# Pooled attention with a layer-normed feed-forward: the last 128 keys multiplied on all rows, another order of heads, smaller pieces

## The chip, the cores and the metric

The kernel runs on 1 core of one Trainium2 chip. The metric is the device time of one execution in microseconds (us), as the median of several runs. The core has a matrix engine (TensorE, rows PE; its weight loads are PEld), VectorE (DVE), ScalarE (ACT), GpSimd (POOL) and an engine that only issues transfers (SP). PE writes its sums to PSUM, a memory of eight banks of 512 floats on each of 128 partitions; DVE and ACT take them from there.

## What is computed

Four batches of eight heads. Queries are averaged in pairs (1152 become 576), then comes ordinary attention with head size 64, and on its output (4 x 576 x 512) a feed-forward layer with layer norm and a residual:

```python
q_pool = q.reshape(B, H, S // 2, 2, D).mean(axis=3)
scores = scale * np.matmul(q_pool, k.transpose(0, 1, 3, 2))
attn = np.exp(scores - np.max(scores, axis=-1, keepdims=True))
attn = attn / (np.sum(attn, axis=-1, keepdims=True) + 1e-09)
x = np.matmul(attn, v)            # then heads side by side: 4 x 576 x 512
xn = (x - mu) / np.sqrt(var + 1e-06) * g_ln
out = x + np.maximum(xn @ w_ch1, 0.0) @ w_ch2      # 512 -> 2048 -> 512
```

Inputs and output are float32. A product of two float32 numbers is made of float16 halves: each factor is split in a high and a low part, and high x high, high x low and low x high are summed.

## The kernel before

**Tiles.** A batch has four pairs of heads (p = 0 to 15 in all), a pair nine score tiles (j = 0 to 8, C = 9), so there are 144 score tiles of 128 queries by 1152 keys. Tile j of a pair belongs to head 0 for j under 4, to head 1 for j over 4; tile 4 holds the last 64 queries of both heads. The output rows of a batch are gathered in `xb[b]`, four groups (t = 0 to 3) of 128 rows by 512 columns; group t needs tile t of each head, so it is whole when the batch's last pair has done its tile for head 1, which is j = 5 for t = 0, j = 6 for t = 1, up to j = 8 for t = 3. The rows of the j = 4 tiles of two batches share one more group (`xh`).

**One step.** `step(i)` writes the work on all engines by hand, in order: DVE's row maximum of tile i (L350), the exponential on ACT (L364), the scores of tile i+1 on PE (`emit_s`, L337), the split of the probabilities into high and low (ACT L378, DVE L387 or POOL L244 and L385), the product with V of an older tile on PE (L433), one piece that prepares the next pair's keys or queries (`a_prep`), and one portion of the feed-forward (`some_units`, at most one a step while tiles are left, two later). Engines run their lists in order.

**Scores.** Keys stand as `kt`, head size on the partitions: keys 0 to 511 of a head on rows 64 to 127, keys 512 to 1151 on rows 0 to 63 (queries `qt` stand on both halves). A tile is nine matmuls over 64 rows: three passes (high-high, high-low, low-high) of two 512-column products, whose two halves of the array run side by side, and then three 128-column products (keys 1024 to 1151) on rows 0 to 63 alone. They have the third bank of the tile's slot, which also holds small outputs, and wait for ACT to read those (L488). For j = 4 each is issued twice at 64 queries.

**The first batch** (`on_pe`, 36 tiles) transposes its probabilities on PE in float32 (L397) and multiplies with V in float32 (L421), while the weights arrive and are split by DVE, ACT and POOL. Later batches transpose by DMA from SP's queue (L390). While tiles of the first batch are worked on, `some_units` is not called.

**Feed-forward.** A whole group is normed (`ln_a`, `ln_r`: DVE L514, POOL L520 to L526), transposed on PE (L532) and split (ACT L538, DVE L539). When two groups (a half of a batch) are through, portions are queued: for each half of the hidden layer (w = 0, 1) four portions of the first product `l1` (L569, 24 matmuls of 256 columns, then ACT L582 and DVE L583 write `ht`), and for each of the two groups two portions of the second product `l2` (L600, 12 matmuls of 512 columns; after the second, DVE L614). So a batch has 32 portions, and the shared groups 8 for two batches.

**Names used below.** Block n is the stretch on PE from the first score matmul of the n-th tile (1 to 144) to that of the next; block 144 holds all that follows.

## Time and profile before

| | us |
|---|---|
| median of 3 runs (892.95 to 897.29) | 895.72 |
| the profiled execution, its own time | 892.43 |
| its span, first to last instruction | 890.6 |
| PE busy, share of the span | 94% |
| DVE, ACT, POOL busy, share of the span | 69%, 64%, 39% |

A row's busy time of PE counts a matmul from its start to its modelled end, and matmuls overlap; what one costs in a stream is the distance of two starts, or the time of a long run of them divided by their number. "Idle before" is time in which the engine waited, with what ended it. PEclk is the granted clock as a share of 2.4 GHz, so 0.50 is 1.2 GHz.

### The profile page before, as it was taken

The numbers are of one execution on the slowest core, as the hardware profiler recorded it, in microseconds if no ns is written. First come the engines' busy times: TensorE is split into PE (matmuls) and PEld (weight loads), VectorE is DVE, ScalarE is ACT, GpSimd is POOL, SyncE is SP. The second block draws the span as 40 slices with busy tenths as digits, with TensorE's granted clock in tenths as the row PEclk, the third lists the DMA queues.
The fourth block names the chain that finished last, engine by engine and source line by source line (L and its number), as shares of the span: only waits on it lengthen the run. The fifth ranks groups of instructions, "written<-read, shape, count | busy, mean of one in ns | idle before, by whom it ended". The sixth has DMA issues, their size and how long they took to land.

```text
span 890.6 us, 22107 instructions
## 1 busy us (share of the span) xinstructions
PE 837.2 (94%) x9430; PEld 608.2 (68%) x9430; DVE 611.8 (69%) x1094; ACT 568.4 (64%) x851; POOL 346.6 (39%) x316
## 2 busy tenths in 40 slices
PE   8898979899799999996999999998999999999997
PEld 6787768677566676754758576676667576776664
DVE  3586988888787777778777777787777777532211
ACT  4888788788677777776677777676767666211110
POOL 3010543543988844336435243535543422300000
PEclk9999999999899999997999999999999999999999
DMA  4554154403498779997896979895979778310001
GB/s 130 196 157 164 50 194 126 172 1 96 92 179 168 141 150 183 180 169 137 154 193 114 203 141 188 127 186 107 222 121 175 129 129 143 57 25 13 13 13 24
DMA packets 271667, 114.95 MB, mean 129 GB/s; under 512 B 254928, under 2 KB 254928, under 8 KB 271568
## 3 DMA queue, kind: packets, MB, share of 16 engines
q1 hardware_dynamic: 271216, 112.65, 61.4%
q8 instruction: 74, 1.21, 0.6%
q10 hardware_dynamic: 352, 0.88, 0.4%
q14 instruction: 25, 0.20, 0.1%
HBM read 45.09 MB, written 4.72 MB: 56 GB/s over the span
## 4 chain that ended last, share of the span: by engine, by line
PE 54%; DVE 25%; ACT 10%; DMA 5%; issue 3%; POOL 2%; SPq 1%; ACTq 0%; POOLq 0%; DVEq 0%
PE psum L569 15%; PE psum L600 15%; DVE mx L350 7%; PE psum L337 7%; PE psum L433 7%; DVE hl L387 4%; PE psum L421 4%; DVE stage L107 3%; ACT pe L364 3%; PE psum L397 2%; DVE ht L583 2%; DVE wsl L107 2%; DVE kt L270 2%; DMA qr<-in_q_dram 2%; DMA kr<-in_k_dram 1%
## 5 line engine op out<-in xcount | busy, mean ns | idle before, releaser
L350 DVE TENSOR_REDUCE mx<-psum 128x1 f32<-128x1152 f32 x144 | 194.2, 1349 | 27.1 <-PE psum L433 18.9
L364 ACT ACTIVATE pe<-psum,nb,sc 128x1152 f32<-128x1152 f32 x144 | 188.9, 1312 | 32.0 <-DVE nb L355 23.6
L600 PE MATMUL psum<-wsl,ht 128*128 128x512 f16 x864 | 196.0, 379 | 0.2 <-DVE ht L583 0.2
L569 PEld LDWEIGHTS <-wsl 128*128 128x128 f16 x1920 | 170.9, 98 | 22.7 <-issue 2.7
L569 PE MATMUL psum<-xn,wsl 128*128 128x256 f16 x1536 | 177.3, 274 | 1.9 <-DVE xn L539 1.0
L337 PE MATMUL psum<-kt,qt 64*128 64x512 f16 (+3 forms) x1440 | 151.8, 332 | 24.7 <-ACT xb L488 13.9
L337 PEld LDWEIGHTS <-qt 64*128 64x128 f16 (+1 forms) x1440 | 70.9, 98 | 116.0 <-issue 66.4
L600 PEld LDWEIGHTS <-ht 128*128 128x128 f16 x864 | 81.8, 98 | 90.0 <-issue 0.4
L378 ACT ACTIVATE hl<-pe 128x1152 f16<-128x1152 f32 x108 | 125.7, 1163 | 5.0 <-DMA pt<-hl 1.6
L433 PE MATMUL psum<-vt,pt 128*128 128x65 f16 (+1 forms) x3240 | 119.8, 195 | 0.0
L433 PEld LDWEIGHTS <-pt 128*128 128x128 f16 (+1 forms) x3240 | 108.1, 101 | 9.4 <-issue 0.6
L488 ACT ACTIVATE xb<-psum,r 128x64 f32<-128x64 f32 x128 | 39.7, 311 | 109.4 <-DVE r L484 100.1
L244 POOL TENSOR_SCALAR pe<-pe 128x1152 f32<-128x1152 f32 x36 | 41.9, 1164 | 164.0 <-ACT hl L378 153.7
L387 DVE SCALAR_TENSOR_TENSOR hl<-pe,hl 128x1152 f16<-128x1152 f32 x72 | 104.3, 1448 | 0.0
L582 ACT ACTIVATE ht<-psum 128x512 f16<-128x512 f32 x72 | 42.7, 594 | 90.6 <-PE psum L569 90.2
L583 DVE SCALAR_TENSOR_TENSOR ht<-psum,ht 128x512 f16<-128x512 f32 x72 | 49.6, 690 | 66.2 <-ACT ht L582 65.4
L385 POOL TENSOR_TENSOR hl<-pe,hl 128x1152 f16<-128x1152 f32 x36 | 86.4, 2400 | 3.0
L421 PE MATMUL psum<-pt,vt 128*65 128x128 f32 (+1 forms) x720 | 81.6, 271 | 0.0
L421 PEld LDWEIGHTS psum<-pt,vt 128*65 128x65 f32 x720 | 75.8, 144 | 0.2 <-issue 0.2
L270 DVE SCALAR_TENSOR_TENSOR qt<-psum,s,qt 128x384 f16<-128x384 f32 x48 | 29.6, 616 | 46.9 <-ACT qt L273 46.9
L270 DVE SCALAR_TENSOR_TENSOR kt<-psum,s,kt 128x512 f16<-128x512 f32 (+1 forms) x48 | 31.5, 658 | 39.1 <-ACT kt L273 39.1
L403 ACT COPY pt<-psum 128x512 f32<-128x512 f32 x72 | 44.9, 639 | 10.8 <-PE psum L397 5.5
(112 smaller groups left out, 925.6 us busy)
## 6 DMA issues: line engine op xcount, KB each, us to landing
stage<-in_moe_w_ch_dram SPq DMA_DIRECT2D x32, 512.0 KB, 5.5
kr<-in_k_dram SPq DMA_DIRECT2D x16, 576.0 KB, 4.7
qr<-in_q_dram SPq DMA_DIRECT2D x31, 288.0 KB, 6.2
vr<-in_v_dram SPq DMA_DIRECT2D x15, 576.0 KB, 4.9
out_dram<-xb SPq DMA_DIRECT2D x32, 128.0 KB, 2.4
pt<-hl SPq DMA_TRANSPOSE x108, 5.0
vr<-in_v_dram ACTq DMA_DIRECT2D x1, 576.0 KB, 6.5
out_dram<-xh SPq DMA_DIRECT2D x4, 128.0 KB, 3.5
```

Source lines behind the costliest of these rows:

```text
L270: nc.vector.scalar_tensor_tensor(lo, ps, s, hi, op0=ALU.mult, op1=ALU.subtract)
L337: nc.tensor.matmul(out=sp[o:o + w, c0:c0 + n], lhsT=qt[r:r + 64, qa, q0:q0 + w], rhs=kt[r:r + 64, ka, h, k0:k0 + n], start=(a == 0), stop= ...
L350: nc.vector.tensor_reduce(mx, st["s"], axis=AX.X, op=ALU.max)
L364: nc.scalar.activation(out=st["pe"], in_=st["s"], func=ACTF.Exp, scale=pair[i // C]["sc"][:, 0:1], bias=st["nb"],)
L378: nc.scalar.activation(out=hl[:, 0], in_=st["pe"], func=ACTF.Copy, scale=2.0 ** 15)
L385: nc.gpsimd.tensor_tensor(hl[:, 1], st["pe"], hl[:, 0], op=ALU.subtract)
L387: nc.vector.scalar_tensor_tensor(hl[:, 1], st["pe"], 2.0 ** 15, hl[:, 0], op0=ALU.mult, op1=ALU.subtract)
L421: nc.tensor.matmul(out=ps[0:65, q0:q0 + w], lhsT=vt[:, h, c], rhs=pt[:, 128 * u + q0:128 * u + q0 + w], start=(u == 0), stop=(u == C - 1),)
L433: nc.tensor.matmul(out=dst[:, 0:n], lhsT=lhsT, rhs=rhs, start=(u == 0 and lhsT is hi and n == 65), stop=(u == C - 1 and lhsT is lo), skip_ ...
L569: nc.tensor.matmul(out=ps[:, o:o + n], lhsT=wsl[:, 8 * w + cc, wa, f * 128:f * 128 + 128], rhs=xn[:, xa * KD + cc, 0:n], start=(m == 0), s ...
L583: lambda: nc.vector.scalar_tensor_tensor(lo, pv, 0.0, hi, op0=ALU.max, op1=ALU.subtract),
L600: nc.tensor.matmul(out=ps, lhsT=hv[0][:, ha, f, t * 128:t * 128 + 128], rhs=wsl[:, 8 * w + 4 + f // 2, wa, (f % 2) * DM:(f % 2) * DM + DM] ...
```

## The change

**Scores.** `kt` keeps 512 keys on each half; the last 128 keys get a place of their own, `k8`, on all 128 rows: rows 0 to 63 hold their high part, rows 64 to 127 their low part. One 128-column matmul over 128 rows then makes high-high and high-low at once, a second one with the queries' low part the rest: eight matmuls a tile for nine. The 512-column products are unchanged. To have the keys on both halves, `kr` gets a tenth column, a second copy of the ninth, with a load of its own on SP's queue (64 KB in runs of 256 bytes for each pair); the PE transpose turns both.

**Order of heads.** `PLACES` names the head and group of each j. In the first two pairs of a batch it is as before; in its last two pairs the heads take turns: (head, t) = (0,0) (1,0) (0,1) (1,1), the shared tile, (0,2) (1,2) (0,3) (1,3). Queries are transposed in that order, and keys of head 1 one place earlier (`PREPS`).

**Pieces.** For the first batch alone, the second product of the second group of each half is made in three portions of 8 matmuls, not two of 12.

**Also.** `all_max` takes its diagonal from the transposed values in PSUM, by one instruction as before.

```diff
+    PLACES = [[(h, t) for h in range(2) for t in range(4)], [(h, t) for t in range(4) for h in range(2)]]
+    for x in PLACES:
+        x.insert(C // 2, None)
...
+        if which == "k":
+            r = raw_p.tile([128, 2, C + 1, D], FP32, tag="kr", name="kr")
+            eng.dma_start(out=r[:, :, 0:C], in_=x)
+            eng.dma_start(out=r[:, :, C], in_=x[:, :, C - 1])
...
-            st["kt"] = tr_p.tile([128, 2, 2, 640], FP16, tag="kt", name="kt")
+            x = tr_p.tile([128, 2304], FP16, tag="kt", name="kt")
+            st["kt"] = x[:, 0:2048].rearrange("p (a h n) -> p a h n", a=2, h=2)
+            st["k8"] = x[:, 2048:2304].rearrange("p (h n) -> p h n", h=2)
...
         for h in range(2):
-            nc.tensor.transpose(ps[0:64, 128 * h:128 * h + 128], kr[:, h, C - 1], ident)
-        x = ps[0:64, 0:256].rearrange("p (h n) -> p h n", h=2)
-        return split_from((p, "k", 2), x, s[0:64, 0:1], kt[0:64, 0, :, 512:640], kt[0:64, 1, :, 512:640])
+            x = kr[:, h, C - 1:C + 1].rearrange("p c d -> p (c d)")
+            nc.tensor.transpose(ps[:, 128 * h:128 * h + 128], x, ident)
+        x = ps[:, 0:256].rearrange("p (h n) -> p h n", h=2)
+        k8 = pair[p]["k8"]
+
+        def low():
+            nc.vector.scalar_tensor_tensor(
+                k8[64:128], x[64:128], s[64:128, 0:1], k8[64:128], op0=ALU.mult, op1=ALU.subtract
+            )
+            have.add((p, "k", 2))
+
+        return (lambda: nc.scalar.activation(out=k8, in_=x, func=ACTF.Copy, scale=s[:, 0:1]), low)
...
-    PREPS = ((prep_k, 0), (prep_k, 2), (prep_q, 0), (prep_q, 1), (prep_k, 1), (prep_q, 2))
+    PREPS = ((prep_k, 0), (prep_k, 2), (prep_q, 0), (prep_k, 1), (prep_q, 1), (prep_q, 2))
...
-        wide = ((64, 0, 512, 0), (0, 512, 512, 0))
-        for here in (wide, ((0, 1024, 128, 512),)):
-            for a, r, c0, n, k0 in [(a, *x) for a in range(3) for x in here]:
-                ka, qa = ((0, 0), (1, 0), (0, 1))[a]
...
+        for a in range(3):
+            ka, qa = ((0, 0), (1, 0), (0, 1))[a]
+            for r, c0 in ((64, 0), (0, 512)):
                 for h, q0, w, o in parts:
                     nc.tensor.matmul(
...
+        for qa in range(2):
+            for h, q0, w, o in parts:
+                nc.tensor.matmul(
+                    out=sp[o:o + w, 1024:1152],
+                    lhsT=qt[:, qa, q0:q0 + w], rhs=pair[p]["k8"][:, h],
+                    start=(qa == 0), stop=(qa == 1),
+                )
...
-            (2 * w + 1, 2 + f0 // 2, lambda t=t, f0=f0: l2(t, f0))
-            for t in range(len(xs)) for f0 in (0, 4)
+            (2 * w + 1, (m1 + 5) // 6, lambda t=t, m0=m0, m1=m1: l2(t, m0, m1))
+            for t in range(len(xs))
+            for m0, m1 in (((0, 8), (8, 16), (16, 24)) if t and fine else ((0, 12), (12, 24)))
...
-                [[(64 * s, rows(b, 2 * x + s)) for s in range(2)] for x in (u, u + 1)],
+                [[(64 * s, rows(b, 2 * x + s)) for s in range(2)] for x in (u, u + 1)], b == 0,
...
-        key = ("h", b // 2) if j == 4 else (b, j if j < 4 else j - 5)
+        key = ("h", b // 2) if j == 4 else (b, PLACES[p % HP // 2][j][1])
```

Where the portions stand after the first batch shows on ACT, which writes `ht` once for each portion of the first product, and casts `xn` once for each normed group. One block is here from one `pe` to the next. Before, from the look at the third pair's values (blocks 39 to 42):

```order
L180 ACTIVATE kt,acc<-vr 128x1152
L916 ACTIVATE pt<-psum,nhalf 65x128
L538 CAST xn<-psum 128x4x128
L364 ACTIVATE pe<-psum,nb,sc 128x1152
L378 ACTIVATE hl<-pe 128x1152
L488 ACTIVATE xb<-psum,r 128x64
L538 CAST xn<-psum 128x4x128
L364 ACTIVATE pe<-psum,nb,sc 128x1152
L378 ACTIVATE hl<-pe 128x1152
L488 ACTIVATE xb<-psum,r 128x64
L273 ACTIVATE kt<-psum,s 128x512
L538 CAST xn<-psum 128x4x128
```

The same place in the changed kernel, from the same instruction on:

```order
L191 ACTIVATE kt,acc<-vr 128x1152
L948 ACTIVATE pt<-psum,nhalf 65x128
L613 ACTIVATE ht<-psum 128x512
L395 ACTIVATE pe<-psum,nb,sc 128x1152
L409 ACTIVATE hl<-pe 128x1152
L519 ACTIVATE xb<-psum,r 128x64
L613 ACTIVATE ht<-psum 128x512
L569 CAST xn<-psum 128x4x128
L395 ACTIVATE pe<-psum,nb,sc 128x1152
L409 ACTIVATE hl<-pe 128x1152
L519 ACTIVATE xb<-psum,r 128x64
L286 ACTIVATE kt<-psum,s 128x512
```

Two of the three casts have gone to earlier blocks, and a portion stands in each block: the first one is in block 40, where before it is in block 43.

The second place is after the first batch's portions (blocks 75 to 79). Before, again from the look at the values of the next pair:

```order
L180 ACTIVATE kt,acc<-vr 128x1152
L488 ACTIVATE xb<-psum,r 128x64
L364 ACTIVATE pe<-psum,nb,sc 128x1152
L378 ACTIVATE hl<-pe 128x1152
L488 ACTIVATE xb<-psum,r 128x64
L538 CAST xn<-psum 128x4x128
L364 ACTIVATE pe<-psum,nb,sc 128x1152
L378 ACTIVATE hl<-pe 128x1152
L488 ACTIVATE xb<-psum,r 128x64
L273 ACTIVATE kt<-psum,s 128x512
L538 CAST xn<-psum 128x4x128
```

And in the changed kernel:

```order
L191 ACTIVATE kt,acc<-vr 128x1152
L519 ACTIVATE xb<-psum,r 128x64
L395 ACTIVATE pe<-psum,nb,sc 128x1152
L409 ACTIVATE hl<-pe 128x1152
L519 ACTIVATE xb<-psum,r 128x64
L613 ACTIVATE ht<-psum 128x512
L395 ACTIVATE pe<-psum,nb,sc 128x1152
L409 ACTIVATE hl<-pe 128x1152
L519 ACTIVATE xb<-psum,r 128x64
L286 ACTIVATE kt<-psum,s 128x512
L613 ACTIVATE ht<-psum 128x512
L569 CAST xn<-psum 128x4x128
```

Before, blocks 75 to 79 have no portion and block 80 the next batch's first; in the changed kernel block 75 has the last piece of the first batch (8 matmuls of the second product), block 76 none, and blocks 77 to 80 one each.

## Rows read from the trace of the kernel before

**Rows 1.** The page: busy time by engine, and the granted clock in 40 slices.

```profile
PE 837.2 (94%) x9430; PEld 608.2 (68%) x9430; DVE 611.8 (69%) x1094; ACT 568.4 (64%) x851; POOL 346.6 (39%) x316
...
PEclk9999999999899999997999999999999999999999
```

**Rows 2.** Busy time by stretch: stretch, its length, engines, clock, DMA share, GB/s.

```profile
core 0: us, PE busy (x) PEld busy (x) DVE busy (x) ACT busy (x) POOL busy (x), PEclk, DMA share, GB/s
14.29:215.25 200.96, 179.34 (x1777) 150.16 (x1778) 161.63 (x262) 161.43 (x296) 64.88 (x52) 0.97 0.38 122
215.25:231.99 16.74, 10.56 (x108) 8.07 (x108) 15.64 (x34) 11.56 (x17) 13.33 (x17) 0.87 0.43 89
231.99:398.40 166.41, 163.72 (x1984) 112.33 (x1983) 122.61 (x221) 119.04 (x161) 105.69 (x77) 0.98 0.87 164
398.40:429.34 30.94, 23.14 (x282) 16.33 (x282) 23.86 (x50) 21.43 (x29) 20.37 (x28) 0.78 0.83 153
429.34:751.09 321.75, 314.47 (x3968) 216.73 (x3968) 241.60 (x440) 226.72 (x303) 129.55 (x113) 1.00 0.84 155
751.09:890.60 139.51, 134.79 (x1179) 94.21 (x1178) 41.84 (x73) 23.24 (x40) 7.97 (x17) 1.00 0.15 29
...
586.98:620.99 34.01, 31.51 (x480) 24.34 (x480) 26.78 (x52) 22.48 (x30) 18.53 (x24) 1.00 0.64 126
...
405.00:412.00 7.00, 6.37 (x61) 4.05 (x60) 5.32 (x14) 5.20 (x8) 6.00 (x9) 0.51 0.74 144
418.70:425.50 6.80, 5.52 (x47) 3.58 (x48) 5.63 (x9) 4.86 (x8) 5.30 (x4) 0.50 0.47 91
217.30:220.70 3.40, 3.22 (x16) 3.02 (x16) 3.04 (x9) 3.37 (x5) 1.29 (x3) 0.50 0.56 117
231.00:237.80 6.80, 5.82 (x49) 4.09 (x49) 5.07 (x10) 5.73 (x7) 6.43 (x9) 0.50 0.93 174
```

**Rows 3.** PE in order of time, one full block: start, length, instruction, count.

```profile
353.00 0.99 PE L337 MATMUL psum<-kt,qt 64*128 64x512 f16 x9
353.92 0.99 PE L433 MATMUL psum<-vt,pt 128*128 128x65 f16 x27
354.74 2.75 PE L600 MATMUL psum<-wsl,ht 128*128 128x512 f16 x12
```

**Rows 4.** The chain that ended last, in the tail: start, length, what.

```profile
781.08 2.68 PE psum L569 x48
...
844.28 10.48 PE psum L569 x96
854.76 10.36 PE psum L600 x48
```

**Rows 5.** Groups by form: busy us, mean ns of one, idle before.

```profile
L433 PE MATMUL psum<-vt,pt 128*128 128x65 f16 x1728 | 97.0, 194 | 0.0
...
L583 DVE SCALAR_TENSOR_TENSOR ht<-psum,ht 128x512 f16<-128x512 f32 x72 | 49.6, 690 | 66.2 <-ACT ht L582 65.4
...
L337 PE MATMUL psum<-kt,qt 64*128 64x128 f16 x384 | 42.6, 218 | 13.6 <-ACT xb L488 12.0 <-ACT xh L488 1.6
...
L270 DVE SCALAR_TENSOR_TENSOR kt<-psum,s,kt 64x256 f16<-64x256 f32 x16 | 7.6, 475 | 9.4 <-ACT kt L273 9.4
```

**Rows 6.** PE in order of time, the block of the first portion.

```profile
231.99 1.78 PE L337 MATMUL psum<-kt,qt 64*128 64x512 f16 x9 [3.67 <-ACT pe L364]
```

**Rows 7.** PE in order of time, blocks 77 to 80.

```profile
404.98 1.81 PE L337 MATMUL psum<-kt,qt 64*64 64x512 f16 x18 [2.82 <-ACT pe L364]
...
419.81 0.63 PE L287 MATMUL psum<-ident,kr 128*64 128x128 f32 x2 [3.92 <-DVE kt L270]
```

**Rows 8.** DMA issues: out<-in, count, KB each, median us to landing.

```profile
kr<-in_k_dram SPq DMA_DIRECT2D x16, 576.0 KB, 4.7
```

**Rows 9.** SP's queue in order of time.

```profile
351.19 0.52 SPq L117 DMA_DIRECT2D kr<-in_k_dram  x1
```

More of the change, by code (lines that the diff above doesn't have):

```diff
@@ L115, in load @@
         src = k if which == "k" else v
-        r = raw_p.tile([128, 2, C, D], FP32, tag=which + "r", name=which + "r")
-        eng.dma_start(out=r, in_=src[b, h:h + 2].rearrange("h (p c) d -> p h c d", c=C))
+        x = src[b, h:h + 2].rearrange("h (p c) d -> p h c d", c=C)
+        if which == "k":
+            r = raw_p.tile([128, 2, C + 1, D], FP32, tag="kr", name="kr")
+            eng.dma_start(out=r[:, :, 0:C], in_=x)
+            eng.dma_start(out=r[:, :, C], in_=x[:, :, C - 1])
+        else:
+            r = raw_p.tile([128, 2, C, D], FP32, tag="vr", name="vr")
+            eng.dma_start(out=r, in_=x)
         raws[p, which] = r
@@ L175, in bound @@
         else:
-            src = raws[p, which][o:o + n].rearrange("p a b d -> p (a b d)")
+            src = raws[p, which][o:o + n, :, 0:C].rearrange("p a b d -> p a (b d)")
             if junk is None:
                 junk = kt_of(p)[o:o + n].rearrange("p a h n -> p (a h n)")[:, 0:S]
+                junk = junk.rearrange("p (a n) -> p a n", a=2)
         m = "kqv".index(which)
@@ L324, in emit_s @@
         if j == 4:
-            parts = [(h, h * C * 64 + 512, 64, 64 * h) for h in range(2)]
+            parts = [(h, 128 * j + 64 * h, 64, 64 * h) for h in range(2)]
         else:
-            h = 0 if j < 4 else 1
-            parts = [(h, h * C * 64 + 128 * (j if h == 0 else j - 5), 128, 0)]
+            parts = [(PLACES[p % HP // 2][j][0], 128 * j, 128, 0)]
         for h, q0, w, o in parts:
@@ L472, in evac_pv @@
                 xb[b] = x_p.tile([128, 4, DM], FP32, tag="xb", name="xb")
[L473 removed]
+            h, t = PLACES[hp // 2][j]
             o, n, m = 0, 128, 1
[L475 removed]
+            x = xb[b][:, t, 128 * hp + 64 * h:128 * hp + 64 * h + 64]
         r = r[o:o + n, 0:m]
@@ L551, in flush, with half_of @@
             drip()
-    def half_of(w, xn, xs, stores, free=()):
+    def half_of(w, xn, xs, stores, fine=False):
         n = 128 * len(xs)
@@ L588, in half_of, with l2 @@
         acc = {}
-        def l2(t, f0):
-            if t == 0 and f0 == 4:
+        def l2(t, m0, m1):
+            if t == 0 and m0 == 12:
                 flush()
-            if f0 == 0:
+            if m0 == 0:
                 acc[t] = bank()
@@ L597, in l2 @@
             ps = acc[t]
-            for f in range(f0, f0 + 4):
-                for ha, wa in ((0, 0), (0, 1), (1, 0)):
-                    nc.tensor.matmul(
-                        out=ps,
-                        lhsT=hv[0][:, ha, f, t * 128:t * 128 + 128],
-                        rhs=wsl[:, 8 * w + 4 + f // 2, wa, (f % 2) * DM:(f % 2) * DM + DM],
-                        start=(f == 0 and ha == 0 and wa == 0),
-                        stop=(f == 7 and ha == 1),
-                    )
-            if f0 == 0:
+            for m in range(m0, m1):
+                f = m // 3
+                ha, wa = ((0, 0), (0, 1), (1, 0))[m % 3]
+                nc.tensor.matmul(
+                    out=ps,
+                    lhsT=hv[0][:, ha, f, t * 128:t * 128 + 128],
+                    rhs=wsl[:, 8 * w + 4 + f // 2, wa, (f % 2) * DM:(f % 2) * DM + DM],
+                    start=(m == 0), stop=(m == 23),
+                )
+            if m1 < 24:
                 return ()
@@ L1021, in tile_pooled_attention_moe @@
         nc.scalar.activation(
-            out=kt_of(0)[:, 0].rearrange("p h n -> p (h n)")[:, 0:C * D],
-            in_=raws[0, "k"][:, 0].rearrange("p c d -> p (c d)"), func=ACTF.Abs,
+            out=kt_of(0).rearrange("p a h n -> p (a h n)")[:, 0:C * D],
+            in_=raws[0, "k"][:, 0, 0:C].rearrange("p c d -> p (c d)"), func=ACTF.Abs,
             accum_out=st["acc"][:, 0:1],
```

26 lines of the change are left out of this document (13 added, 13 removed).

## The prediction

> **What bounds the kernel now.** I read the page first: PE is busy 94% of the span and no other engine over 69% [rows 1]. That is an average, so next the stretches [rows 2]. In blocks 43 to 74 and 81 to 143 PE is busy 163.72 of 166.41 and 314.47 of 321.75 us, both 98%: a microsecond taken from PE there comes off the time. The tail (from block 144) is PE alone too, 134.79 of 139.51; its long runs of the two products follow each other without a hole [rows 4]. PE is not the limit in three places. Blocks 1 to 39, the first batch's attention: PE 179.34 of 200.96. Blocks 40 to 42: PE 10.56 of 16.74, DVE 15.64 of it. Blocks 75 to 80: PE 23.14 of 30.94, DVE 23.86. In the last two PE has its scores and its product with V but no portion of the feed-forward: the first batch's are not there yet, or are used up while the second's wait for their norms. PE stands for ACT or DVE, 2.82 and 3.92 us at a time [rows 7], and 3.67 at the end of the first hole [rows 6]. After pauses of PE the granted clock is down: 0.51, 0.50, 0.50 and 0.50 in the last four stretches of [rows 2], 1.2 GHz, so that a score tile takes 1.78 us [rows 6] for 0.99 [rows 3]. Where PE has work, half of such a stretch is lost to it: 3.4 us of the last one.
>
> **A matmul's price.** Busy time of one doesn't price it: 218 ns for a 128-column score matmul [rows 5]. Starts do. A run of 48 matmuls of 128 columns takes 2.68 us, 56 ns each; 96 of 256 columns 10.48, 109 ns each; 48 of 512 columns 10.36, 216 ns each [rows 4]. The block of [rows 3] fits: 0.92 us from scores to the product with V is 3 x 0.216 + 3 x 0.056 = 0.82, and some 0.10 left over, where the matmuls go from 128 rows to 64 and back. A portion of the first product is 24 x 0.109 = 2.62 us, one of the second 12 x 0.216 = 2.59, a small one 8 x 0.216 = 1.73.
>
> The Trainium skill, page "Trainium Kernel Development and Optimization", section Performance Expectations, says that matmul busy time is a bad metric since matmuls are pipelined. This trace agrees: 160 matmuls fewer would be worth 160 x 0.218 = 34.9 us by their busy time and 9.0 by their starts.
>
> **Scores on all rows.** 160 matmuls of 128 columns go (1440 to 1280), one a tile, two half-wide ones for j = 4. I take 0.056 us a tile. The three old ones stand on rows 0 to 63 alone, nothing runs beside them, and a matmul over 128 rows costs the same 56 ns [rows 4]. The passage from 64 to 128 rows now lies before the short products, not behind them; it is one passage either way. Bounds: 0 (the passage costs 0.05 more in its new place) and 0.15 (it vanishes where the short products wait anyway). Both ends count in PE-bound blocks.
>
> **Its preparation.** Instructions stay one for one on PE, ACT and DVE; at worst the split on DVE costs twice, another 7.6 us over 16 pairs [rows 5], on an engine that is 69 to 75% busy where PE bounds. Nothing. The second load costs SP 0.5 us per pair [rows 9]; behind it stand that block's transposes of probabilities, whose reader on PE never waited (idle 0.0) [rows 5]. Nothing while that slack holds. The keys of head 1 are turned one block earlier, so `kr` comes free earlier: a gain, if any. The diagonal of `all_max` is one small instruction either way.
>
> **Order of heads, pieces.** Group 1 of a batch is whole three tiles earlier (j = 3 for 6), so its portions start three blocks earlier: block 40 for 43, block 77 for 80 (the order above). The first batch has 36 portions for 32 (four sets of 3 pieces for 2). Work is the same; what changes is how many blocks lie without any. By stretch:
>
> Blocks 40 to 42 gain three portions of the first product, 7.9 us. PE has 10.56 busy in 16.74, 3.22 of it at half clock [rows 2], so its own work at full clock is 9.0; two norm transposes of 0.5 move forward, which with the portions makes 15.9. DVE has 15.64; it loses the work of two norms and gains three halves of `ht` at 0.69 [rows 5]. So the portions nearly fill the hole and the stretch stays about as long, 16.5: **-0.2**. Bounds: -0.9, and +3 if they don't fit by a third.
>
> Blocks 43 to 74 lose 3 x 2.62 + 1.73 = 9.6 (the portions done before, and 8 matmuls that move behind), and 32 x 0.056 = 1.8; they gain a norm's transposes, 0.5. Of the 3.4 lost at half clock at their start I take half back, 1.7. Against it: in a dozen blocks with a small piece PE has 3.4 to 4 us of work, while DVE needs 122.6 / 32 = 3.8 on average [rows 2]. So DVE ends some of them: +2 (0 to 4). **-10.6** (-14.3 to -5, the latter without the scores' gain and the clock's).
>
> Blocks 75 to 80 gain the 9.6 back. PE's 23.14 holds 6.37 + 5.52 = 11.9 at half clock [rows 2], so it is 17.2 at full, 26.8 with the portions. DVE's 23.86 gains four halves of `ht`, 2.8, and loses about as much, since the norms now come every other block and not four in a row. I take 28 for 30.94: **-3** (-4 to +1).
>
> Blocks 81 to 143 keep one portion each: 63 x 0.056 = 3.5, and something of the 2.5 us in which PE idles around the next norms (586.98 to 620.99) [rows 2]: **-4** (-5 to -1).
>
> The tail has three portions fewer: **-8**. This is the surest term; the order gives the count, 600 for 672 matmuls of the first product.
>
> Blocks 1 to 39: at most 39 x 0.056 = 2.2 from the scores, a little more where the short products wait for L488; against it two norms moved in here, some 3 us of DVE, 1 of PE. **0** (-3 to +2.5).
>
> Sum: -0.2 - 10.6 - 3 - 4 - 8 = -25.8. From the profiled execution's own 892.43 that is 866.6. The median of the runs stands 3.3 above that execution, so 870 for the median. All best ends (-0.9, -14.3, -4, -5, -8, -3) give -35.2, 860; all worst (+3, -5, +1, -1, -8, +2.5) give -7.5, 888.
>
> **Rivals.** (1) The holes don't take the portions: DVE is at 93% in blocks 40 to 42 and 77% in 75 to 80, and a portion comes with work for DVE and ACT, behind which the next row maximum waits. For it: PE's waits there end on ACT and DVE [rows 6, 7]. Against it: the stretch from 586.98 has norms and portions together, and PE is busy 31.51 of 34.01. Price: +3 in the first hole, +4 in light blocks, +1 in the second, half the gain of the scores gone, 4: some 11 us less, 881 at the median.
>
> (2) The change doesn't shorten the score tile: a 128-row weight load must wait until both halves of the array are through, and the two short products cost as much as three. For it: 0.10 us of each block is already spent on such a passage. Against it: the product with V streams 27 such matmuls in 0.82 us, 30 ns each [rows 3]. Price: the 0.056 of 134 blocks or so, 7.5: 877.
>
> (3) Clock: if PE no longer pauses long in the two holes, the clock stays up, and stretch for stretch the best ends come true: 861. For it: PE had paused ahead of the slow stretches of both holes [rows 6, 7]. Against it: DVE still limits there.
>
> (4) Slower than before: the second load of keys delays the transposes by DMA. The DMA engines are busy 0.83 to 0.87 of blocks 43 to 143 [rows 2], and the load comes in the same short stretch as a load of keys, values and queries. Price: to lose 25.8 us and 4.5 more, PE must wait 2.5 us for each of the 12 loads that meet such transposes, beyond the slack that it has now. Against it: the load has a ninth of the bytes of the one beside it, which takes 4.7 us to land [rows 8]; even as much again for each pair would have to go past the slack. It decides only if the small runs cost several times what the long ones do. That gives 897 or more.
>
> On those runs the Trainium skill, page "DMA: Bandwidth & Descriptors", section Specifications, asks for 512 bytes or more per transfer and says that below this the engine reads, modifies and writes; the new load has 256. No row of this trace shows such a load of keys. By that rule rival (4) would gain, and the time would be 897 or more.
>
> **How the numbers follow.** Forecast, 870: 0.66. Rival (1), 881: 0.14. Rival (2), 877: 0.07. Rival (3), 861: 0.07. No change, where holes and scores both give nothing and only the tail's blocks move: 0.03. Rival (4): 0.03. The range 858 to 882 takes in the forecast's bounds and rivals (1) to (3) nearly whole, and leaves out the last two and the tails of the sum, under 2 in 10. A measurement of this kernel can tell about 0.5%, 4.5 us, from no change. Faster by more: the forecast and rivals (1) to (3), less a little, 0.93; within: 0.04; slower: 0.03.
>
> **What would show it.** In the changed kernel's trace: eight score matmuls in about 0.87 us from the first to the product with V; portions in blocks 40 to 42 and 77 to 79, with blocks 40 to 42 about as long as before; PE's first portion of the second batch some 11 us earlier against its old place plus the gains before it; a tail shorter by 8; fewer stretches at half clock. I am wrong if blocks 40 to 42 or 75 to 80 grow by several us, if light blocks end on DVE for more than 4 us in sum, if PE begins to wait for transposed tiles, or if a score tile still takes 0.92.

## The result, and the profile after

The changed kernel takes **885.85 us** in the median (4 runs, 883.11 to 887.93), the kernel before 896.5 beside it: ratio **0.9891**, 95% interval 0.9859 to 0.9923 (the two medians alone give 0.988). The sign was right, the size was not: 870 was forecast, 858 to 882 was the range, and 10.6 us came where 25.8 were expected. The profiled execution took 883.11 us (span 881.3), against 892.43 (890.6) before.

The page after the change, PE's busy time and the granted clock; they answer to [rows 1]:

```profile
PE 826.2 (94%) x9270; PEld 586.0 (66%) x9270; DVE 613.4 (70%) x1092; ACT 568.7 (65%) x851; POOL 348.7 (40%) x318
...
PEclk9999989999999999999999999999999999999999
```

PE's busy time fell by 11 us, and in this execution the clock is up from block 40 on. The same stretches as in [rows 2], after the change: blocks 1 to 39, 40 to 42, 43 to 74, 75 to 80, 81 to 143, and the tail. Columns as there.

```profile
core 0: us, PE busy (x) PEld busy (x) DVE busy (x) ACT busy (x) POOL busy (x), PEclk, DMA share, GB/s
15.34:214.32 198.98, 179.08 (x1744) 147.86 (x1744) 163.54 (x267) 161.84 (x298) 67.51 (x60) 0.96 0.40 127
214.32:231.78 17.46, 15.67 (x167) 12.33 (x167) 12.72 (x27) 13.01 (x18) 11.66 (x12) 1.00 0.55 103
231.78:398.31 166.53, 152.48 (x1874) 99.16 (x1874) 128.46 (x226) 116.23 (x156) 108.09 (x84) 1.00 0.83 159
398.31:428.65 30.34, 26.92 (x350) 19.87 (x350) 23.30 (x48) 23.52 (x33) 15.86 (x19) 1.00 0.89 157
428.65:750.00 321.35, 313.06 (x3898) 208.20 (x3898) 242.62 (x442) 226.52 (x300) 132.37 (x117) 1.00 0.85 157
750.00:881.30 131.30, 126.66 (x1106) 87.07 (x1105) 37.70 (x66) 22.56 (x39) 7.93 (x16) 1.00 0.15 32
```

The third row is the riddle: PE has 11.2 us less to do there (163.72 before) and the stretch is as long as before (166.41). PE stands for 14.0 us in it, where it stood for 2.7. Of the waits over 0.5 us, 11.2 us in sum (1.6 before), 7.3 end on DVE (2.79, 0.86, 0.88 and 1.17 in blocks 43, 46, 47 and 49, 1.57 in block 73) and 3.9 on ACT's look at the keys and values of the next pair (1.40 in block 50, 2.54 in block 68). Set against the terms of the prediction, all in profiled executions:

| blocks | forecast | measured |
|---|---|---|
| start of the first score | none | +1.1 |
| 1 to 39 | 0 | -2.0 |
| 40 to 42 | -0.2 | +0.7 |
| 43 to 74 | -10.6 | +0.1 |
| 75 to 80 | -3 | -0.6 |
| 81 to 143 | -4 | -0.4 |
| tail | -8 | -8.2 |
| sum | -25.8 | -9.3 |

Two terms hold the miss: 43 to 74, and the scores in 81 to 143.

**Where PE stands in block 68.** This is the longest wait for a load. First SP's queue: four loads of queries, then transposes, the keys and the values of the next pair.

```profile
338.53 2.68 SPq L421 DMA_TRANSPOSE pt<-hl  x1
341.26 2.86 SPq L137 DMA_DIRECT2D qr<-in_q_dram  x4
...
345.58 4.77 SPq L421 DMA_TRANSPOSE pt<-hl  x1
350.79 0.39 SPq L121 DMA_DIRECT2D kr<-in_k_dram  x1
...
351.81 4.50 SPq L421 DMA_TRANSPOSE pt<-hl  x1
356.36 0.58 SPq L125 DMA_DIRECT2D vr<-in_v_dram  x1
```

Then ACT, which looks for the largest key and value, and PE's turn of what it found (`all_max`, L207):

```profile
355.85 1.16 ACT L191 ACTIVATE kt<-kr 128x1152 f16<-128x1152 f32 x1 [2.26 <-DMA kr<-in_k_dram]
...
361.27 1.16 ACT L191 ACTIVATE kt<-vr 128x1152 f16<-128x1152 f32 x1 [0.42 <-DMA vr<-in_v_dram]
...
362.58 0.27 PE L207 MATMUL psum<-ident,acc 128*3 128x128 f32 x1 [2.54 <-ACT kt L191]
```

A transpose behind the query loads holds SP for 4.8 and 4.5 us where 2.7 did before them, so the keys are issued at 350.79. In the kernel before they were issued at 351.19 [rows 9], but there PE was 2.4 us further back: block 66 began at 353.00 [rows 3], after the change at 350.62. PE runs ahead, the loads do not. The blocks 64 to 68 themselves, after the change, each from one tile's scores to the next:

```profile
341.34:346.49 5.15, 5.15 (x78) 3.26 (x78) 4.59 (x8) 2.58 (x3) 1.69 (x2) 1.00 1.03 222
346.49:350.62 4.13, 4.13 (x50) 2.34 (x50) 2.48 (x5) 3.57 (x7) 2.58 (x2) 1.00 1.13 202
350.62:354.14 3.52, 3.52 (x45) 1.85 (x45) 2.92 (x3) 2.94 (x4) 3.46 (x2) 1.00 1.00 245
354.14:358.97 4.83, 4.56 (x60) 3.47 (x59) 4.72 (x9) 3.09 (x5) 0.59 (x1) 1.00 1.09 180
358.97:366.22 7.25, 4.71 (x69) 3.58 (x69) 3.16 (x10) 6.20 (x9) 3.65 (x3) 1.00 1.12 218
```

Blocks 66 and 68 before:

```profile
353.00:357.43 4.43, 4.43 (x50) 2.36 (x50) 3.85 (x6) 3.74 (x6) 3.02 (x2) 1.00 1.06 287
...
361.89:366.64 4.75, 4.65 (x71) 3.71 (x71) 2.85 (x7) 4.12 (x6) 1.70 (x2) 1.00 1.22 184
```

The last column but one is the DMA share: it is full, 1.00 to 1.13, in the blocks that small pieces have shortened to 3.5 and 4.1 us. (A packet counts where it starts, so a short stretch can show more than 1.) It was as full before, but PE then had 4.4 us of work in block 66 and stood for 0.1 us in block 68. DVE (4.59 of 5.15 and 4.72 of 4.83 us) and POOL (3.46 of 3.52) are near their limits in single blocks too, so three bounds lie close under PE's there; the one that PE waits for is in the last row.

**Where PE stands in blocks 43 to 49.** POOL, DVE and PE, in block 43 and then in block 48:

```profile
232.06 2.13 POOL L788 TENSOR_TENSOR wsl<-wsl 128x1024 f16<-128x1024 f32 x1
232.21 2.07 DVE L246 TENSOR_SCALAR s<-s 128x3 f32<-128x3 f32 x1
...
236.43 0.44 PE L301 MATMUL psum<-ident,kr 128*128 128x128 f32 x2 [2.79 <-DVE kt L283]
...
262.20 2.63 POOL L172 TENSOR_TENSOR qr<-qr 128x1152 f32<-128x1152 f32 x1
262.41 0.62 DVE L283 SCALAR_TENSOR_TENSOR qt<-psum,s,qt 128x384 f16<-128x384 f32 x1 [0.91 <-ACT qt L286]
262.94 3.10 DVE L418 SCALAR_TENSOR_TENSOR hl<-pe,hl 128x1152 f16<-128x1152 f32 x1
```

An instruction of three columns takes 2.07 us on DVE, from just after POOL's split of weights starts until it ends; the split of a tile takes 3.10 beside POOL's sum of queries and 1.35 where POOL is idle. PE's waits of 2.79, 0.86, 0.88 and 1.17 us in blocks 43, 46, 47 and 49 end on DVE; `bare` below shows how many of them go with POOL's splits.

**The score tile.** PE in order of time, first with the product with V behind the scores, then with a matmul of three rows:

```profile
350.62 0.82 PE L362 MATMUL psum<-kt,qt 64*128 64x512 f16 x6
351.38 0.29 PE L370 MATMUL psum<-kt,qt 128*128 128x128 f16 x2
351.50 0.98 PE L464 MATMUL psum<-vt,pt 128*128 128x65 f16 x27
...
366.22 0.82 PE L362 MATMUL psum<-kt,qt 64*128 64x512 f16 x6
366.98 0.29 PE L370 MATMUL psum<-kt,qt 128*128 128x128 f16 x2
367.19 0.38 PE L218 MATMUL psum<-dg,ones 3*128 3x3 f32 x2
```

0.88 us from the first score to the product with V, for 0.92 in [rows 3]: what was forecast. But 0.97 where L218 follows. The passage from 64 rows to 128 shows as well: 0.76 from the first wide matmul to the first short one, where three wide pairs of 0.216 are 0.65.

### The profile page after: what moved, and what is told of

Same layout as the page of the kernel before. It is cut to its first block, busy times and chain, and to the rows that moved or that the text cites. A ratio compares the mean times of both kernels' runs of the same rounds, so it can differ in the third digit from the quotient of the medians.

```text
span 881.3 us, 21831 instructions
## 1 busy us (share of the span) xinstructions
PE 826.2 (94%) x9270; PEld 586.0 (66%) x9270; DVE 613.4 (70%) x1092; ACT 568.7 (65%) x851; POOL 348.7 (40%) x318
## 3 DMA queue, kind: packets, MB, share of 16 engines
HBM read 46.14 MB, written 4.72 MB: 58 GB/s over the span
## 4 chain that ended last, share of the span: by engine, by line
PE 47%; DVE 24%; ACT 11%; DMA 6%; issue 6%; POOL 4%; SPq 1%; ACTq 0%; POOLq 0%; DVEq 0%
PE psum L600 15%; PE psum L632 13%; DVE mx L381 7%; PE psum L464 5%; PE psum L362 4%; DVE hl L418 4%; PE psum L452 3%; ACT pe L395 3%; DVE stage L109 3%; DMA qr<-in_q_dram 2%; PE psum L428 2%; DVE ht L614 2%; DVE wsl L109 1%; PE psum L370 1%; DMA stage<-in_moe_w_ch_dram 1%
## 5 line engine op out<-in xcount | busy, mean ns | idle before, releaser
L362 PE MATMUL psum<-kt,qt 64*128 64x512 f16 (+1 forms) x960 | 122.4, 382 | 0.7 <-ACT pe L395 0.7
L464 PE MATMUL psum<-vt,pt 128*128 128x65 f16 (+1 forms) x3240 | 117.0, 193 | 0.0
L418 DVE SCALAR_TENSOR_TENSOR hl<-pe,hl 128x1152 f16<-128x1152 f32 x72 | 108.9, 1512 | 0.0
L362 PEld LDWEIGHTS <-qt 64*128 64x128 f16 (+1 forms) x960 | 34.2, 96 | 53.3 <-issue 35.6
L370 PEld LDWEIGHTS <-qt 128*128 128x128 f16 (+1 forms) x320 | 17.9, 99 | 73.4 <-issue 72.9
L370 PE MATMUL psum<-kt,qt 128*128 128x128 f16 (+1 forms) x320 | 41.3, 226 | 12.6 <-ACT xb L519 11.0
```

Source lines behind the costliest of these rows:

```text
L362: nc.tensor.matmul(out=sp[o:o + w, c0:c0 + 512], lhsT=qt[r:r + 64, qa, q0:q0 + w], rhs=kt[r:r + 64, ka, h], start=(a == 0), stop=(a == 2),)
L370: nc.tensor.matmul(out=sp[o:o + w, 1024:1152], lhsT=qt[:, qa, q0:q0 + w], rhs=pair[p]["k8"][:, h], start=(qa == 0), stop=(qa == 1),)
L418: nc.vector.scalar_tensor_tensor(hl[:, 1], st["pe"], 2.0 ** 15, hl[:, 0], op0=ALU.mult, op1=ALU.subtract)
L464: nc.tensor.matmul(out=dst[:, 0:n], lhsT=lhsT, rhs=rhs, start=(u == 0 and lhsT is hi and n == 65), stop=(u == C - 1 and lhsT is lo), skip_ ...
```

## The experiments

Theories after the result. **L**: the loads of the next pairs don't come sooner when PE does, and PE waits for them. **P**: POOL's splits of weights hold up DVE. **C**: where PE has little to do, the tile's own work on ACT, DVE and POOL ends the block, whatever is loaded or split. Ratios are to the kernel before on the same chip; differences in us between versions are of their medians.

### One part at a time

`scores_only` has the new scores, with the old order and portions:

```diff
-    PLACES = [[(h, t) for h in range(2) for t in range(4)], [(h, t) for t in range(4) for h in range(2)]]
+    PLACES = [[(h, t) for h in range(2) for t in range(4)], [(h, t) for h in range(2) for t in range(4)]]
...
-    PREPS = ((prep_k, 0), (prep_k, 2), (prep_q, 0), (prep_k, 1), (prep_q, 1), (prep_q, 2))
+    PREPS = ((prep_k, 0), (prep_k, 2), (prep_q, 0), (prep_q, 1), (prep_k, 1), (prep_q, 2))
...
-                [[(64 * s, rows(b, 2 * x + s)) for s in range(2)] for x in (u, u + 1)], b == 0,
+                [[(64 * s, rows(b, 2 * x + s)) for s in range(2)] for x in (u, u + 1)], False,
```

> The kernel before with the change of the scores alone (keys 1024 to 1151 on 128 rows, the second load of keys), heads and pieces as before. Theory A (the freed PE time is lost to other engines; a score tile does get shorter): by the changed kernel's trace a tile is 45 ns shorter where the product with V follows, 50 ns longer where the broadcast of all_max follows and some 70 to 170 ns longer in the shared tile, so 2 to 3 us off, ratio 0.997. Theory B (my recorded price, 56 ns in each PE-bound block): 7.5 us off, ratio 0.992. Theory C (the second load or the passage to 128 rows costs what the matmul saves): ratio 1.000 or above.

`heads_only` has the new order alone: the last line of that diff, and the scores as before.

> The kernel before with the order of heads alone (and the keys of head 1 turned one place earlier), scores and pieces as before. Three portions move from the tail to blocks 40 to 42; the hole of five blocks without a portion stays, three blocks earlier. Theory A: the tail is 8 us shorter, but blocks 43 to 56 give back part of it, since DVE and POOL end them: 4 to 6 us off, ratio 0.994. Theory B (PE-bound all through): 8 us off, ratio 0.991.

`heads_pieces` has order and pieces, the scores as before.

> Order of heads and small pieces, scores as before: against heads_only this fills four of the five empty blocks with portions of the first batch. Theory A: the pieces lighten blocks that PE no longer ends, so they add 0 to 2 us at most: 5 to 8 us off, ratio 0.993. Theory B: another 8 to 10 us off, 17 in all, ratio 0.981.

The changed kernel ran again beside them.

> The changed kernel once more, on the chip of the other three, for their differences: ratio 0.989 as measured. If the parts add up, scores_only and heads_pieces together give it.

Measured: scores_only 893.0 us, ratio 0.9979 (0.9954 to 1.0005); heads_only 888.29, 0.9909 (0.9880 to 0.9939); heads_pieces 886.92, 0.9896 (0.9862 to 0.9930); the changed kernel again 886.47, 0.9889 (0.9855 to 0.9924). So the order of heads makes nearly the whole gain, about 8 us, all of it in the tail (131.41 us there in heads_only's trace); the scores, at some 2, and the pieces, which were to fill in what the portions had left in blocks 43 to 74, at about 1, are too small for the intervals: that of scores_only takes in 1, and those of heads_only and heads_pieces overlap. Block by block the traces show that they do work and are then undone: heads_pieces reaches block 67 at 356.39 us, heads_only at 361.71, 5.3 us later. By block 77 heads_pieces is 1.0 us behind; its execution has 3.4 us of half clock more than that of heads_only in block 43 and as much in block 68.

In the repeated run of the changed kernel the wait in block 68 is followed by half clock:

```profile
359.60:369.53 9.93, 7.41 (x68) 5.20 (x68) 2.94 (x7) 6.90 (x10) 3.65 (x3) 0.66 1.20 232
```

Granted clock 0.66 of 2.4 GHz as a mean of the block, 1.2 GHz for two thirds of it; 9.93 us for 7.25 above. heads_pieces has it too, for 3.4 us (block 68: 8.51). So this wait costs 2.5 us, or 5 where the clock falls after it.

### Loads and splits moved

`loads_early` issues the four query loads of two pairs ten steps earlier, from the seventh pair on (p = 6; the expectations say the fifth, here and below):

```diff
-            at(i0 - 2, load_q, p, (nc.sync,))
+            at(i0 - (12 if p > 4 else 2), load_q, p, (nc.sync,))
```

> The changed kernel, with the four query loads of each two pairs issued ten steps earlier from the fifth pair on (1.15 MB; for block 64's pair in blocks 51 to 53, where the DMA engines are busy 0.44 to 0.69, instead of blocks 62 to 64). Theory L (the loads of the next pairs take the gain: the DMA engines are full, share 1.00 to 1.13, in blocks 64 to 69, keys and values come late, ACT reads them late, and PE waits with L207 for ACT): PE's waits at L207 of 1.40, 2.54, 1.36, 0.99 and 0.82 us in blocks 50, 68, 77, 104 and 122, 7.1 in sum, go for the most part; 5 us less than the changed kernel, ratio to the kernel before 0.983 to 0.985. Theory C (in blocks with little for PE, the tile's own chain over ACT, DVE and POOL ends the block): the waits get another releaser, at most 1 us less, ratio 0.988 to 0.990.

`splits_early` begins POOL's splits of the weights' third quarter as soon as they can be made:

```diff
-            i0 = this[0] + 1 + 3 * n // 2 if part < 2 else 16 + 10 * part + 5 * n // 2
+            i0 = this[0] + 1 + 3 * n // 2 if part < 3 else 16 + 10 * part + 5 * n // 2
```

> The changed kernel, with POOL's splits of the third quarter of the weights begun as soon as their scale is known (some five blocks earlier, in blocks 31 to 38) and not in blocks 37 to 46. Theory P (POOL's splits beside DVE make both slow, and so hold up blocks 43 to 49): the wait of 2.79 us in block 43 goes and those of 0.86, 0.88 and 1.17 in blocks 46 to 49 shrink; blocks 43 to 56 take 73 us for 76.4, ratio to the kernel before 0.985. Theory C (ACT, DVE and the transposes have no room there anyway): blocks 43 to 56 within 1 us of 76.4, ratio 0.988 to 0.990.

`both_early` has both edits.

> Both moves at once in the changed kernel. L and P both true: the gains add, some 8 to 9 us less than the changed kernel, ratio to the kernel before 0.979 to 0.981. Only one true: 0.983 to 0.986. Theory C: 0.988 to 0.990, and blocks 43 to 74 still 165 us or more.

`before_loads` is the kernel before with the edit of the loads.

> The kernel before, with the same earlier query loads and nothing else. Theory L: PE has work in every block there, so the full DMA engines of blocks 46 to 50 and 64 to 69 cost only the small waits at L196 (0.85, 0.89 and 1.06 us in blocks 50, 86 and 122): 1 to 2 us less, ratio 0.998 to 0.999. If it is 0.995 or less, the place of the loads costs the kernel before as much as the changed one, and does not explain where the gain of the pieces went.

Measured: loads_early 882.89 us, 0.9864 (0.9844 to 0.9884); splits_early 885.98, 0.9899 (0.9873 to 0.9926); both_early 884.13, 0.9872 (0.9852 to 0.9893); before_loads 890.97, 0.9947 (0.9926 to 0.9967).

The loads: about half of what L expected. The wait of block 68 falls from 2.54 to 0.67 us, those of blocks 104 and 122 from 0.99 and 0.82 to 0.29 and 0.32, but a new one stands in block 59, where the queries now run into the keys and values of the pair between:

```profile
321.08 0.27 PE L207 MATMUL psum<-ident,acc 128*3 128x128 f32 x1 [2.29 <-ACT kt L191]
```

The splits: block 43 takes 6.14 us for 7.95 and 44 to 49 29.79 for 31.58, as P says; blocks 34 to 36, where they now stand, take 18.36 for 16.46 and blocks 40 to 42 18.96 for 17.46, and the wait of block 50 grows from 1.40 to 1.94, of block 68 from 2.54 to 2.92. Nothing is left (885.98 us for 886.47 on the same chip). With both, blocks 43 to 74 take 160.46 us for 166.53, and blocks 1 to 39 203.89 for 198.98: the gain is there and is paid for ahead of it.

The control went against L by its own terms: the kernel before gains 0.5% from earlier loads as well, more than its waits for them (0.85 us in block 50, 0.89 in 86, 1.06 in 122) account for. The traces (spans 892.2 and 890.6) can't show it: the profiled execution of before_loads, 894.03 us, is the slowest of its ten, and that of the kernel before lies 3.3 under the median of its runs. So a comparison with the kernel before can't tell what loads do to the pieces. That takes pairs of kernels that differ in the pieces alone.

### With the suspects taken out, and the loads spread

`bare` loads no queries from the seventh pair on and takes those of an earlier pair again, and uses the first half of the weights in place of the second, which POOL doesn't split:

```diff
     def load_q(p, engs, us=(0, 1)):
+        if p > 4:
+            raws[p, "q"] = raws[p + 1, "q"] = raws[p - 4, "q"]
+            return
...
-                            lhsT=wsl[:, 8 * w + cc, wa, f * 128:f * 128 + 128],
+                            lhsT=wsl[:, cc, wa, f * 128:f * 128 + 128],
...
     def w_split_a(n):
+        if n > 7:
+            return
```

> The changed kernel with both suspected causes taken out: from the fifth pair on no queries are loaded (those of earlier pairs are used again, so the output is not the reference's), and POOL doesn't split the second half of the weights (the first half's stand in for it). All matmuls, their order and the work of ACT and DVE are as in the changed kernel. Theory LP (loads and POOL's splits held PE up where the pieces made room): PE's waits at L207 and those of blocks 43 to 49 go, blocks 43 to 74 take 156 us or less for 166.5, and this kernel is 7 to 10 us faster than the same without pieces (bare_nopieces); ratio to the kernel before some 0.973 to 0.977. Theory C (ACT, DVE and POOL's work of each tile ends the light blocks): other waits take their place, blocks 43 to 74 take 160 us or more, and it is at most 3 us faster than without pieces; ratio 0.979 to 0.984.

> The same, without the smaller pieces (the second product of each group in two portions of 12, as before the change). Both theories: loads and splits cost this kernel less, since PE has work in each block; ratio to the kernel before 0.982 to 0.986. What counts is the difference to bare: 7 to 10 us by LP, at most 3 by C.

`spread` distributes the four loads, two early and two late:

```diff
-            at(i0 - 2, load_q, p, (nc.sync,))
+            if p < 6:
+                at(i0 - 2, load_q, p, (nc.sync,))
+            for n in range(4 if p > 4 else 0):
+                at(i0 - (14, 13, 5, 4)[n], q_part, p, n)
```

> The changed kernel with the four query loads of each two pairs spread from the fifth pair on: two ten steps before the loads of the pair between, two shortly after them, so that no step has all four. Theory L: the wait of 2.29 us in block 59, which the loads ten steps earlier had brought, is not there, and those at L207 of 2.54, 0.99 and 0.82 us in blocks 68, 104 and 122 fall to about 0.6, 0.3 and 0.3; 4 us less than the changed kernel, ratio to the kernel before 0.984 to 0.986. Otherwise the wait moves again, and the ratio stays at 0.986 to 0.989.

> The kernel before with the same spread loads and nothing else. With all four loads ten steps earlier it gained 0.5%. If that came from the loads' place, it shows again: 0.993 to 0.997. If it was chance, 0.998 to 1.001.

> The changed kernel with spread query loads, without the smaller pieces. With loads and splits both out of the way the pieces gave 4.9 us. Here POOL's splits are still there, which hold up blocks 43 to 49: if they take the rest, the pieces are worth 1 to 3 us, ratio to the kernel before 0.982 to 0.984 (0.981 with pieces). If the loads were what mattered, they are worth 4 to 5 us, 0.985 to 0.987.

Measured: bare 875.71 us, 0.9761 (0.9731 to 0.9792); bare_nopieces 880.62, 0.9816 (0.9787 to 0.9846); **spread 879.25, 0.9810** (0.9778 to 0.9841); before_spread 891.82, 0.9943 (0.9922 to 0.9963); spread_nopieces 886.78, 0.9906 (0.9873 to 0.9938), the last on another chip than spread, and slower than either expectation had it. spread is the best version that computes the whole: 6.6 us under the changed kernel, 17 under the kernel before. L had expected 4 of these 6.6. The spans of the profiled executions differ by 3.4, and 3.0 of that lies in blocks 43 to 74; the half clock that can follow the wait of block 68, which neither of these two executions has there, may be the rest.

SP, and PE in block 68, in spread:

```profile
347.50 0.52 SPq L121 DMA_DIRECT2D kr<-in_k_dram  x1
...
352.96 0.37 SPq L125 DMA_DIRECT2D vr<-in_v_dram  x1
```

```profile
360.66 0.27 PE L218 MATMUL psum<-ident,acc 128*3 128x128 f32 x1 [0.67 <-ACT kt L202]
```

Keys and values are issued 3.3 and 3.4 us earlier than in the changed kernel, the wait of block 68 is down to 0.67, and block 59 has none. Blocks 43 to 74 of spread and of spread_nopieces:

```profile
232.85:396.38 163.53, 153.41 (x1874) 99.83 (x1873) 128.01 (x226) 115.88 (x156) 106.97 (x84) 0.99 0.84 162
```

```profile
232.93:400.73 167.80, 155.96 (x1883) 101.39 (x1882) 127.54 (x224) 114.68 (x155) 104.64 (x83) 0.98 0.84 158
```

Blocks 75 to 80 add 30.35 and 33.51 us, so by block 80 the pieces are worth 7.4 us in these traces, and 0.8 in those of heads_pieces and heads_only (197.62 for 198.42). By the ratios of whole runs it is some 8 to 9 us for 1. The two that share a chip, bare and bare_nopieces, differ by 4.9 us in the medians, and no run of one reaches those of the other; their blocks 43 to 74 and 75 to 80:

```profile
231.19:389.57 158.38, 152.06 (x1874) 99.04 (x1874) 121.56 (x226) 115.78 (x156) 73.15 (x65) 1.00 0.79 153
389.57:421.41 31.84, 28.53 (x350) 20.98 (x349) 23.30 (x48) 23.71 (x33) 15.84 (x19) 0.95 0.75 150
```

```profile
231.90:394.47 162.57, 154.18 (x1883) 100.78 (x1882) 121.51 (x224) 114.62 (x155) 71.74 (x64) 0.98 0.82 147
394.47:428.46 33.99, 30.25 (x342) 21.86 (x342) 23.93 (x51) 25.07 (x34) 16.61 (x21) 0.83 0.73 149
```

That is 6.3 us, between the two theories. What follows for the pieces: they are worth 5 to 8 us if queries are not loaded where they are, with POOL's splits there or not, and about 1 (measured with the old scores) if they are. So the place of the loads decides what the pieces bring. One thing in this is open: with the pieces out, moved loads gain nothing (heads_only 0.9909, spread_nopieces, with the new scores, 0.9906), while they gain 0.5% in the kernel before, and no run shows why.

What follows for blocks 43 to 74 of the changed kernel: 166.53 us fall to 163.53 with the loads spread, all of it in blocks 50 to 74 (127.00 to 124.00; blocks 43 to 49 take 39.53 in both, in spread with 3.4 us at half clock). They fall to 158.38 with loads and splits gone, and 4.1 of these further 5 us lie in blocks 43 to 49 (35.39), where the waits of blocks 46, 47 and 49 go and that of block 43 falls to 0.98. DVE does the same 226 instructions there in 121.56 us for 128.46. The splits cost the kernel without pieces as much (167.80 and 162.57). And C has a share: in bare, with both gone, PE still waits 0.98 us in block 43, 0.65 in 50, 0.67 in 68 and 1.56 in 73 for DVE and ACT.

Why the kernel before gains 0.5% from moved loads is not settled: both versions of it say so, and the span of before_spread, 890.4 us in an execution near its median, is that of the kernel before in a fast one.

### Splits and scores on top of spread

`spread_splits` starts the splits of the third quarter five blocks earlier, at their old distances.

```diff
-            i0 = this[0] + 1 + 3 * n // 2 if part < 2 else 16 + 10 * part + 5 * n // 2
+            i0 = this[0] + 1 + 3 * n // 2 if part < 2 else (11 if part == 2 else 16) + 10 * part + 5 * n // 2
```

> The changed kernel with spread query loads and POOL's splits of the third quarter of the weights five blocks earlier at their old distances. Theory P: the wait of 2.79 us in block 43 falls under 1 and blocks 43 to 49 take 3 us less; at their former earlier place they had cost 1.9 us in blocks 34 to 36, here up to 2; net 1 to 3 us less, ratio 0.978 to 0.980. If what the splits cost is the same wherever they stand: 0.981 to 0.983, the time lost in blocks 31 to 39.

This one and the next two ran on another chip than spread. Measured: 882.82 us, 0.9861 (0.9829 to 0.9894), 0.5% above spread, with overlapping intervals. Blocks 44 to 49 take 28.41 us for spread's 30.39, but another split meets DVE in block 43 now, so the wait there stays at 2.78, and blocks 34 to 39 pay. In spread_splits they are, and then in the changed kernel (29.32 in spread):

```profile
185.84:220.95 35.11, 28.42 (x252) 23.35 (x252) 28.20 (x41) 21.89 (x41) 25.09 (x29) 0.90 0.21 53
```

```profile
184.99:214.32 29.33, 25.35 (x253) 20.04 (x253) 25.71 (x41) 21.92 (x41) 15.34 (x21) 1.00 0.19 51
```

5.8 us more, with the clock down to 0.90. The splits cost time in each of the three places tried.

`spread_noscores` is spread with the scores as before the change.

> The changed kernel with spread query loads and the scores as before the change (nine matmuls a tile). By the price in the prediction, 56 ns a tile, the new scores are worth some 7 us, ratio 0.989. By the starts in the changed kernel's trace (45 ns less where the product with V follows, 50 to 180 ns more where a matmul of few rows follows, some 20 ns a tile on average) they are worth 2 to 3 us, ratio 0.983 to 0.985, and blocks 81 to 143 take some 1.2 us more than the 319.85 with the new scores. Worth nothing: 0.980 to 0.982.

Measured: 880.96 us, 0.9841 (0.9805 to 0.9878) for 0.9810. That is the ratio which 2 to 3 us would give, but the intervals overlap. The traces part them, block by block. Block 94, without and with the new scores:

```profile
495.48 0.99 PE L358 MATMUL psum<-kt,qt 64*128 64x512 f16 x9
496.40 0.99 PE L454 MATMUL psum<-vt,pt 128*128 128x65 f16 x27
497.24 2.78 PE L590 MATMUL psum<-xn,wsl 128*128 128x256 f16 x24
```

```profile
493.71 0.82 PE L373 MATMUL psum<-kt,qt 64*128 64x512 f16 x6
494.47 0.28 PE L381 MATMUL psum<-kt,qt 128*128 128x128 f16 x2
494.59 0.98 PE L475 MATMUL psum<-vt,pt 128*128 128x65 f16 x27
495.41 2.78 PE L611 MATMUL psum<-xn,wsl 128*128 128x256 f16 x24
```

From start to start the block takes 4.464 and 4.404 us, and 29 of the 63 blocks 81 to 143 are shorter by 45 to 65 ns: the forecast's 56. But 18 are longer by 40 to 75 ns. In 12 of these a three-row matmul or a product with 64-column weights follows, and 0.21 us lie between the first short matmul and it, for 0.12; five more are the shared tile's own, and one has neither. Twelve differ by under 40 ns, four by more. The sum over the 63 blocks is -0.2 us.

`narrow_first` puts the two short products ahead of the six wide ones in each tile.

> The changed kernel with spread query loads and the two short products of a score tile ahead of the six wide ones. If a passage between 128 and 64 rows costs the same some 95 ns wherever it stands, a block is as long as before this move: within 1 us in sum, ratio 0.980 to 0.982, and only blocks with a matmul of few rows behind the scores change, by 50 ns to either side. If the short products, now first, wait for ACT's reading of the bank that they share with small outputs, PE gets new waits ahead of them and the time grows by 3 us or more, 0.985 or more.

Measured: 893.14 us, 0.9976 (0.9953 to 1.0000). Not the passage: blocks 43 to 80 are as in spread (193.8 us, spread 193.9), 81 to 143 take 319.2 for 319.85. Blocks 1 to 39 take 212.87 for 200.00. There the short products wait for ACT to read the small outputs out of their bank. The groups of short products, in narrow_first and in the changed kernel (busy, mean ns | idle before):

```profile
L371 PE MATMUL psum<-kt,qt 128*128 128x128 f16 x256 | 35.5, 220 | 23.1 <-ACT xb L530 17.1 <-ACT xh L530 4.2 <-DVE kt L317 0.7
```

```profile
L370 PE MATMUL psum<-kt,qt 128*128 128x128 f16 x256 | 36.5, 224 | 11.5 <-ACT xb L519 9.9 <-ACT xh L519 0.9 <-DVE stage L109 0.6
```

23.1 us of waiting for 11.5. The wide products in front had been covering that read.

## Why the prediction was right or wrong

**Blocks 43 to 74, -10.6: this step failed.** The work on PE went as counted (11.2 us less busy time), and no clock was lost there in the profiled execution. What failed was "a microsecond taken from PE there comes off the time", drawn from PE's 98%: the microseconds taken became waits, 14.0 us for 2.7. The 98% left 2.7 us of slack in 166, and the lightened blocks were the very ones in which POOL splits weights beside DVE (43 to 49), or keys, values and queries for the next pairs arrive and the DMA engines are full. The mean DMA share of the stretch, 0.87 [rows 2], hid blocks at 1.0 and more. Spreading the loads gave back 3.0 us of the stretch; with loads and splits both out it takes 158.38, 8.0 under the kernel before, so these two hold most of the 10.6. I gave +2 for light blocks and looked for their end at DVE's average alone, 3.8 us a block. Rival (1) had the mechanism, portions that don't pay since others end the block, with a price of +4 there and the work that portions bring for ACT and DVE as the culprit; 7.3 us of the waits do end on DVE, but 4.7 of them go when POOL's splits go, and the loads, which rival (1) left out, come next. (Its prices add up to 12 us, not the 11 that it gives.) Rival (4) looked at loads, but at the new small one of keys, for which nothing speaks: in the changed kernel the 64 KB land in 4.3 us (median), the 576 KB beside them in 4.6.

**Blocks 81 to 143, -4, and the scores' 56 ns.** The price was right for half of the blocks. It was carried to all of them, though the trace of before listed what follows the scores in each. As measured in the pair spread and spread_noscores, the term is -0.2; whether the new scores gain the rest of scores_only's 2 us in earlier blocks, the runs don't show. The bound of 0, "the passage costs 0.05 more in its new place", was passed in 18 of 63 blocks, which got longer.

**Blocks 75 to 80, -3: +2.4 off.** The half clock went, as said. But PE waits 1.36 us for ACT's look at the next pair's values in block 77 and 1.07 for POOL in block 78.

**Right:** the tail, -8.2 for -8, from counting portions. The first hole: the portions fit and the stretch stays about as long (+0.7). The clock of rival (3) came true from block 40 on in the profiled execution, without its gain, since the time it would have given back was spent waiting. Blocks 1 to 39 at -2.0 lie within their bounds; two norms cost 3.1 us in blocks 34 to 39 (29.3 for 26.2), and the first five blocks, with 1.5 us at half clock for 3.4, gave nearly as much back (21.36 for 24.29). That was not forecast, so that the term came out near 0 is in part luck; but it is not chance, for all versions with the new order have it (20.7 to 21.9).

**The range** took in bounds term by term. With the worst ends on record for the three terms that missed, -5, +1 and -1, the sum is -13.2 and the time 882.5. What came lies beyond the first and the third: +0.1 and -0.4. Both bounds counted what PE saves and let a part of it go; neither was made from the next bound itself: POOL's splits and the loads in the first, the neighbours in the second.

## What to carry to other kernels

An engine that is busy for 98% of a stretch says what bounds it now, not how much of its work may go before another bound is met: before pricing a saving, read the DMA share, the other engines and the waits block by block, and compare the time at which each load is issued with the time at which the faster engine would want it. When work is made lighter in some places, move the loads that are tied to those places with it. A price per instruction holds for the neighbours with which it was read; count how many places have other neighbours.

## What the runs showed of the hardware

A VectorE instruction of 128 x 3 took 2.07 us instead of 0.17 beside a GpSimd instruction of 2.13 us, and the split of a tile 3.10 instead of 1.35. An instruction whose large operand lies in PSUM beside the same kind of work took its usual time: the split of queries at 262.41 us 0.62, beside GpSimd's sum that then held the tile's split to 3.10. The Trainium skill, page "SBUF — State Buffer", section "SBUF: two separate sides", says that the two engines share one pair of ports which whoever comes first holds for its whole instruction, against VectorE instructions with two operands in SBUF or in a two-port mode. The traces here agree for the tile's split, both of whose operands lie in SBUF; in which mode the 128 x 3 instruction ran no row shows.

A PE wait of 2.4 to 2.9 us in block 68 was followed by 1.2 GHz in two of four profiled executions (3.4 us in heads_pieces, 6.8 in the repeated run of the changed kernel) and not in the others (the changed kernel's first, and splits_early). Block 43 is alike: nine versions wait 2.77 to 2.79 us in it, four of them keep 2.4 GHz and take 7.94 to 7.99 us, and five have 3.4 to 6.8 us at 1.2 GHz and take 9.14 to 10.49. It is the pause's second price, and it differs from execution to execution.
